# Layer 2 in two passes over halves of DFF, its first product by Strassen's scheme

## The chip, the cores and the metric

The kernel runs on one core of one Trainium2 chip. The metric is the device time of one execution in microseconds. One execution was also taken with the hardware profiler; all rows of the trace are from that one. Its engines are called PE (TensorE), DVE (VectorE), ACT (ScalarE), POOL (GpSimd) and SP (SyncE, which here only issues DMAs).

## The reference, cut to what matters

Attention over 4 x 576 tokens with a memory term gives 2304 tokens of 512. Two layers follow, each a product with a 512 x 2048 matrix, a function of each element, and a product with a 2048 x 512 matrix. The change touches the second of them.

```python
def _moe_ref(x, w_in, w_out, s, b):          # layer 1
    r = np.maximum(x @ w_in, 0.0)
    return (s * (r * r) + b) @ w_out

def _moe2_ref(x, w_in, w_out):               # layer 2
    h = x @ w_in
    g = np.where(h >= 1.0, h, np.where(h <= -1.0, 0.0, (h + 1.0) ** 2 / 4.0))
    return g @ w_out
```

The weights come as 64-bit floats and are converted on the chip.

## The kernel before, in words

**Arithmetic.** Matrix operands are split into a high and a low part of the type float32r (`rnd` rounds, `sub` subtracts the high part), and each product is made of three matmuls: high x high, high x low, low x high. So a product of one 128 x 128 weight tile with a stretch of tokens is three matmuls, each with its own weight load.

**Stages.** Attention and layer 1 are interleaved (`ORDER`, line 44): layer 1 takes blocks of 256 tokens, its last, block 7, has 512. Its output goes to DRAM (`x2d`) and comes back for layer 2. In layer 1 all of layer 1's weights lie in SBUF, in 32 tiles of 512 KB (`wi0` to `wi15`, `wo0` to `wo15`). During block 7 each of them is replaced, as soon as its last reader is done, by the converted and split tile of layer 2 (`fetch_w`, `split_w`). A conversion is one scaling, one step on the low words and two bitwise steps on VectorE (lines 603 to 614).

**Layer 2** (`layer2`, line 953) takes six blocks of 384 tokens (`T2`). For each of 16 tiles of 128 of DFF: the first product in 4 x 3 matmuls of 384 columns into a PSUM bank (`h_mms`, lines 851 to 853), then the bend on two engines (clip on VectorE, L1000; square on ScalarE, L507; maximum on VectorE, L1002; rounding, L522; subtraction, L514), then 3 x 3 matmuls of 512 columns into three banks that collect the output (L1008, L1009, L1012). After the 16th tile these banks go through SBUF to `out`. x for the next block is loaded and split meanwhile into the other half of `xh` and `xl` (`jx`).

**What sets the order.** The program is a list of operations with what they read and write. `Plan` (line 108) places them one by one on the engines' queues by its own table of costs and hand-over times, so that each engine has a fixed order; an operation may be offered to two or three engines (`rnd`: ScalarE, VectorE, GpSimd; `sub`: VectorE, GpSimd). Operations of VectorE on SBUF and those of GpSimd are not planned at the same time; operations that read PSUM are marked `alone` and are free of that rule. Buffers come from a `Pool`; most pools hand out their units in the order of the program. PSUM has 8 banks: four serve the first product in layer 2 and four the output (`hand_over`, line 945). Where the plan has a gap on PE it puts matmuls on zeros (L1035).

```python
953  def layer2(bi):
956      jx = bi % 2
989      for fi in range(NF):
991          h_mms(fi, hs, n, lambda kt: xh2(kt), lambda kt: xl2(kt), ...)
1000         dve(c_dve(n), alone(... tensor_scalar(a_(), hv(), -1.0, 1.0, ALU.max, ALU.min)), [hs], [r], FFN, [r])
```

## Time and profile before

| | us |
|---|---|
| median of 3 runs (lowest, highest) | 1027.61 (1026.58, 1027.63) |
| the profiled execution, its whole time | 1032.56 |
| its span, first to last instruction | 1030.4 |
| PE busy in the span | 1016.9 |
| DVE busy | 578.3 |
| ACT busy | 535.1 |
| POOL busy | 149.9 |

Busy time is the sum of the times at which an engine had an instruction in work. Matmuls overlap in the array, so a PE that is always busy may still be slower than it could be; how fast it goes is read from the distance between the starts of two matmuls. PEld is the weight load that goes with each matmul. A row's "idle before" is the time that the engine stood still ahead of such instructions, with what ended it.

### The profile page before, as it was taken

What the parts mean: (1) busy time and instruction counts of PE and PEld (TensorE: products, weight loads), DVE (VectorE), ACT (ScalarE), POOL (GpSimd) and SP (SyncE); (2) the same over time, 40 slices, a digit from 0 to 9 for tenths busy, and PEclk for the clock granted to TensorE, in tenths of its full rate; (3) what the DMA queues carried; (4) which work ended last, traced back from release to release, by engine and by line L of the source; (5) the groups of instructions that cost most, each with busy time, mean ns of one, the idle gap of its engine ahead of it and who ended that gap; (6) DMA issues with size and microseconds to landing.
All of it is one profiled execution on the core that took longest, in us unless ns stands there. A gap on an engine that the chain in (4) does not pass through costs nothing.

```text
span 1030.4 us, 18179 instructions
## 1 busy us (share of the span) xinstructions
PE 1016.9 (99%) x7100; PEld 901.2 (87%) x7100; DVE 578.3 (56%) x1425; ACT 535.1 (52%) x1246; POOL 149.9 (15%) x249
## 2 busy tenths in 40 slices
PE   7999999999999999999999999999999999999997
PEld 6799998898898898898997889999999999999996
DVE  5899865625645635634888885343343443534433
...
PEclk8999999999999999999999999999999999999999
...
GB/s 310 185 411 31 20 96 147 62 35 80 65 53 76 46 75 62 60 65 22 93 164 152 193 106 133 1 62 1 1 62 1 1 31 1 31 1 1 31 1 31
DMA packets 32630, 77.20 MB, mean 75 GB/s; under 512 B 3232, under 2 KB 12448, under 8 KB 32544
## 3 DMA queue, kind: packets, MB, share of 16 engines
...
## 4 chain that ended last, share of the span: by engine, by line
PE 91%; ACT 4%; DVE 2%; DMA 2%; issue 0%; POOL 0%; SPq 0%; ACTq 0%; POOLq 0%; DVEq 0%
PE hb L851 9%; PE hb L852 9%; PE hb L853 9%; PE ab L726 6%; PE yb L914 5%; PE yb L919 5%; PE yb L915 5%; PE ab L805 4%; PE ab L781 4%; PE ab L1009 4%; PE ab L1008 4%; PE ab L1012 3%; PE ab L852 3%; PE ab L851 3%; PE ab L853 3%; PE yb L1008 3%
## 5 line engine op out<-in xcount | busy, mean ns | idle before, releaser
L851 PE MATMUL hb<-xh,wi 128*128 128x256 f32 (+2 forms) x704 | 217.7, 309 | 0.1
L852 PE MATMUL hb<-xl,wi 128*128 128x256 f32 (+2 forms) x704 | 214.6, 305 | 0.0
L853 PE MATMUL hb<-xh,wi 128*128 128x256 f32 (+2 forms) x704 | 214.4, 305 | 0.0
L507 ACT ACTIVATE r<-r,con 128x384 f32<-128x384 f32 x96 | 59.2, 617 | 201.2 <-DVE r L1000 201.1
L851 PEld LDWEIGHTS hb<-xh,wi 128*128 128x128 f32 x704 | 132.5, 188 | 8.2 <-issue 3.5
L852 PEld LDWEIGHTS hb<-xl,wi 128*128 128x128 f32 x704 | 132.3, 188 | 3.8
L853 PEld LDWEIGHTS hb<-xh,wi 128*128 128x128 f32 x704 | 132.2, 188 | 2.9
L914 PE MATMUL yb<-gg,wo 128*128 128x256 f32 (+1 forms) x396 | 103.0, 292 | 0.6 <-ACT gg L522 0.6
L915 PE MATMUL yb<-gg,wo 128*128 128x256 f32 (+1 forms) x396 | 98.8, 282 | 0.0
L507 ACT ACTIVATE aa<-aa,sm 128x384 f32<-128x384 f32 (+4 forms) x112 | 69.8, 624 | 47.9 <-DVE sm L737 47.6
L522 ACT ACTIVATE g<-r 128x384 fp32r<-128x384 f32 x96 | 50.5, 526 | 67.3 <-DVE r L1002 67.3
L514 DVE TENSOR_TENSOR gg<-rr,gg 128x256 fp32r<-128x256 f32 x100 | 43.9, 440 | 72.9 <-ACT gg L522 55.2
L914 PEld LDWEIGHTS yb<-gg,wo 128*128 128x128 f32 x396 | 74.5, 188 | 8.0 <-issue 3.6
L737 DVE CUSTOM_DVE_ANT_0 aa<-ab,mask 128x512 f32<-128x512 f32 (+3 forms) x112 | 59.1, 554 | 32.8 <-PE ab L726 32.5
L915 PEld LDWEIGHTS yb<-gg,wo 128*128 128x128 f32 x396 | 74.6, 188 | 0.6
L1000 DVE TENSOR_SCALAR r<-hb 128x384 f32<-128x384 f32 x48 | 26.7, 557 | 79.6 <-PE hb L853 79.5
L919 PE MATMUL yb<-gg,wo 128*128 128x256 f32 (+1 forms) x396 | 69.8, 289 | 0.0
L514 DVE TENSOR_TENSOR g<-r,g 128x384 fp32r<-128x384 f32 x92 | 51.0, 554 | 29.6 <-ACT g L522 29.4
L896 ACT ACTIVATE rr<-hb 128x256 f32<-128x256 f32 x97 | 38.7, 399 | 51.7 <-PE hb L853 50.7
L851 PE MATMUL ab<-xh,wi 128*128 128x384 f32 x192 | 64.9, 338 | 0.0
L852 PE MATMUL ab<-xl,wi 128*128 128x384 f32 x192 | 64.9, 338 | 0.0
L853 PE MATMUL ab<-xh,wi 128*128 128x384 f32 x192 | 64.8, 338 | 0.0
...
## 6 DMA issues: line engine op xcount, KB each, us to landing
...
wir<-in_moe_w_in_dram SPq DMA_DIRECT2D x16, 512.0 KB, 10.3
wor<-in_moe_w_out_dram SPq DMA_DIRECT2D x16, 512.0 KB, 10.2
raw<-in_moe_w_in_dram SPq DMA_DIRECT2D x16, 512.0 KB, 4.0
raw<-in_moe_w_out_dram SPq DMA_DIRECT2D x16, 512.0 KB, 3.7
...
```

The lines of the kernel that those rows point to most:

```text
L507: nc.scalar.activation(o(), i(), func, **{a: b() if callable(b) else b for a, b in kw.items()})
L514: ways = [("DVE", c_dve(n), lambda: nc.vector.tensor_tensor(o(), a(), f(hi()), ALU.subtract))]
L522: ways = [("ACT", c_act(n, 0, psum), lambda: nc.scalar.activation(o(), a(), AF.Copy)), ("DVE", c_dve(n, "tt" if psum else "cp"), lambda: n ...
L726: nc.tensor.matmul(zs[x].t[own if t == 4 else slice(0, n), at:at + c1 - c0], qk.t[own, q0:q0 + n], qk.t[own, k0 + c0:k0 + c1], start=True, ...
L737: dve(c_dve(c1 - c0) + 0.02, alone(lambda a=a, s=s, z=zs[x], c0=c0, c1=c1, m0=m0, pi=pi, j=j, at=at, ao=ao: nc.vector.tensor_tensor_reduce ...
L851: nc.tensor.matmul(o, w_in_part(fi, 0)[:, kt, :], x_h(kt), start=kt == 0, stop=False)
L852: nc.tensor.matmul(o, w_in_part(fi, 0)[:, kt, :], x_l(kt), start=False, stop=False)
L853: nc.tensor.matmul(o, w_in_part(fi, 1)[:, kt, :], x_h(kt), start=False, stop=kt == NK - 1)
L914: nc.tensor.matmul(yv(c), w_out_part(fi, 0)[:, cs], gg.t[0], start=fi == 0 and c % k == 0, stop=False)
L915: nc.tensor.matmul(yv(c), w_out_part(fi, 1)[:, cs], gg.t[0], start=False, stop=False)
L919: pe(c_mm(n), lambda c=c, cs=cs, gg=gg, fi=fi: nc.tensor.matmul(yv(c), w_out_part(fi, 0)[:, cs], gg.t[1], start=False, stop=fi == NF - 1 a ...
L1008: nc.tensor.matmul(ys[c].t, gg.t[0][:, cs], w_out_part(fi, 0), start=fi == 0, stop=False)
```

## The change

Layer 2 makes two passes over all tokens, each with one half of DFF. The first pass leaves its sums in DRAM (`yd`), the second adds its own to them and writes `out`. Blocks have 512 tokens, but for one of 256. For a block of 512, two tiles of DFF (256) and the 512 of x are taken as 2 x 2 matrices of half size, and the first product is made by Strassen's scheme in Winograd's form: seven products with sums of quarters of the weights (`prepare` makes them once) and of x (`x2_sums` makes them for every block and pass), and seven additions on VectorE (`plus`). A group is two such pairs, side by side in one PSUM bank. The block of 256 is done as before, with 256 columns (`plain`). The sums of the weights for the second pass are made during the first and put down in DRAM (`w2d`); `bring` loads them over those of the first pass. The passes go through the blocks as 0 1 2 3 4 and 4 1 2 3 0, so that block 4 keeps its x.

```diff
-T2 = 384
+
+HALF = NF // 4
...
-BLOCKS2 = [(i * T2, (i + 1) * T2) for i in range(NTOK // T2)]
+FIRST, SECOND = (0, 1, 2, 3, 4), (4, 1, 2, 3, 0)
+BLOCKS2 = [(0, T)] + [(T + 2 * T * i, T + 2 * T * (i + 1)) for i in range(4)]
...
+    def prepare(p):
+
+        q, later = p % HALF, p >= HALF
+        plan.phase = 1
+
+        def put(k, make):
+
+            nm, i, j = home(q, k)
+            if not later:
+                make(lambda: part(nm, i, j), home_key(q, k), [])
+                return
+            sg = R_STG2.take()
+            make(lambda: sg.t.bitcast(F32R), sg, [sg])
+            dma(lambda: w2d[p, k // 2][:, 512 * j:512 * j + 512], lambda: sg.t, P * 2048, [sg], [f"w2d{p}_{k // 2}"], W2)
+
+        def split(k, a, r):
+            def make(o, key, acq):
+                rnd(lambda: o()[:, 0:256], a, 256, r, [key], W2, acq=acq)
+                sub(lambda: o()[:, 256:512], a, lambda: o()[:, 0:256], 256, r, [key], W2)
+            put(k, make)
+
+        c1, c2 = fetch_2("wi", 2 * p), fetch_2("wi", 2 * p + 1)
+        ta, tb = R_STG2.take(), R_STG2.take()
+
+        def v(x, j):
+            return lambda: x.t[:, 256 * j:256 * j + 256]
+
+        def tt(o, a, b, op, r, w, acq):
+            add([("DVE", c_dve(256), lambda: nc.vector.tensor_tensor(o(), a(), b(), op)),
+                 ("POOL", c_pool(256, "tt"), lambda: nc.gpsimd.tensor_tensor(o(), a(), b(), op))], r, w, W2, acq)
+        tt(v(ta, 0), v(c2, 0), v(c2, 1), ALU.add, [c2], [(ta, 0)], [ta])
+        tt(v(ta, 1), v(ta, 0), v(c1, 0), ALU.subtract, [(ta, 0), c1], [(ta, 1)], [])
+        tt(v(tb, 0), v(c1, 0), v(c2, 0), ALU.subtract, [c1, c2], [(tb, 0)], [tb])
+        tt(v(tb, 1), v(c1, 1), v(ta, 1), ALU.subtract, [c1, (ta, 1)], [(tb, 1)], [])
+        for k, a, r in ((0, v(c1, 0), c1), (4, v(ta, 0), (ta, 0)), (5, v(ta, 1), (ta, 1)), (3, v(c2, 1), c2), (6, v(tb, 0), (tb, 0)),
+                        (1, v(c1, 1), c1), (2, v(tb, 1), (tb, 1)), (7, v(c2, 0), c2)):
+            split(k, a, [r])
+        for i in range(2):
+            st = fetch_2("wo", 2 * p + i)
+            if not later:
+                o, l = (lambda i=i: wo2(q, i, 0)), (lambda i=i: wo2(q, i, 1))
+                rnd(o, lambda st=st: st.t, 512, [st], [home_key(q, 8 + 2 * i)], W2)
+                sub(l, lambda st=st: st.t, o, 512, [st, home_key(q, 8 + 2 * i)], [home_key(q, 9 + 2 * i)], W2)
+                continue
+            for k in (8 + 2 * i, 9 + 2 * i):
+                sg = R_STG2.take()
+                if k % 2 == 0:
+                    hi = sg
+                    rnd(lambda sg=sg: sg.t.bitcast(F32R), lambda st=st: st.t, 512, [st], [sg], W2, acq=[sg])
+                else:
+                    add([("DVE", c_dve(512), lambda sg=sg, st=st, hi=hi: nc.vector.tensor_tensor(sg.t.bitcast(F32R), st.t, hi.t, ALU.subtract)),
+                         ("POOL", c_pool(512, "tt"), lambda sg=sg, st=st, hi=hi: nc.gpsimd.tensor_tensor(sg.t.bitcast(F32R), st.t, hi.t, ALU.subtract))],
+                        [st, hi], [sg], W2, [sg])
+                dma(lambda k=k: w2d[p, k // 2][:, 512 * (k % 2):512 * (k % 2) + 512], lambda sg=sg: sg.t, P * 2048, [sg], [f"w2d{p}_{k // 2}"], W2)
+        plan.phase = None
...
+    def bring(p):
+
+        for k in range(0, 12, 2):
+            nm, i, _ = home(p % HALF, k)
+            dma(lambda nm=nm, i=i: f(parts_t[nm, i]), lambda k=k: w2d[p, k // 2], P * 4096, [f"w2d{p}_{k // 2}"],
+                [f"{nm}h{i}", f"{nm}l{i}"], W2)
...
+            if len(BLOCKS) - 1 in blocks and fi % 3 == 2 and fi < 3 * HALF:
+                prepare(fi // 3)
...
+    def x2_sums(bi):
+
+        def xr():
+            return made["xr"].rearrange("p (c n) -> p c n", c=NK)
+        load_x2(bi, xr)
+        for kt in range(NK):
+            def xv(kt=kt):
+                return xr()[:, kt]
+            add([("ACT", c_act(512, 1), lambda kt=kt, xv=xv: nc.scalar.activation(xv(), xv(), AF.Identity, bias=col(kt))),
+                 ("DVE", c_dve(512, "cp"), lambda kt=kt, xv=xv: nc.vector.tensor_scalar(xv(), xv(), col(kt), None, ALU.add)),
+                 ("POOL", c_pool(512), lambda kt=kt, xv=xv: nc.gpsimd.tensor_scalar(xv(), xv(), col(kt), 1.0, ALU.add, ALU.mult))],
+                ["xr", "cs"], [f"xr{kt // 2}{j}" for j in range(2)], FFN)
+
+        def b(i, j):
+            return lambda: xr()[:, 2 * i:2 * i + 2, T * j:T * j + T]
+
+        def tt(i, j, a, c):
+            o = b(i, j)
+            add([("DVE", c_dve(512), lambda: nc.vector.tensor_tensor(o(), b(*a)(), b(*c)(), ALU.subtract)),
+                 ("POOL", c_pool(512, "tt"), lambda: nc.gpsimd.tensor_tensor(o(), b(*a)(), b(*c)(), ALU.subtract))],
+                ["xr"] + [f"xr{i}{j}" for i, j in (a, c)], [f"xr{i}{j}"], FFN)
+
+        def halves(k, i, j):
+            a, r = b(i, j), ["xr", f"xr{i}{j}"]
+
+            def hi():
+                return xo_all(k, 0).rearrange("p (c n) -> p c n", c=2)
+
+            def lo():
+                return xo_all(k, 1).rearrange("p (c n) -> p c n", c=2)
+            rnd(hi, a, 512, r + [free_of(k)], [f"xo{k}"], FFN)
+            sub(lo, a, hi, 512, r, [f"xo{k}"], FFN)
+        halves(0, 0, 0)
+        tt(0, 0, (0, 1), (0, 0))
+        halves(4, 0, 0)
+        tt(0, 0, (1, 1), (0, 0))
+        halves(5, 0, 0)
+        tt(0, 1, (1, 1), (0, 1))
+        halves(6, 0, 1)
+        halves(1, 1, 0)
+        tt(1, 0, (1, 0), (0, 0))
+        halves(3, 1, 0)
+        halves(2, 1, 1)
...
+    def bend(c, h):
+
+        gh, gl, x = R_G.take(), R_G.take(), R_C.take()
+
+        def tmp():
+            return x.t
+
+        def cv():
+            return c.t
+        src = c if h is None else h
+        clip = lambda: nc.vector.tensor_scalar(tmp(), src.t, -1.0, 1.0, ALU.max, ALU.min)
+        dve(c_dve(512, "cp" if h is None else "tt"), clip if h is None else alone(clip), [src, "wide"], [x], FFN, [x])
+        act(tmp, tmp, AF.Square, 512, ["sb"], [x], FFN, ap=1, scale=0.5, bias=con[:, 4:5])
+        if h is None:
+            dve(c_dve(512), lambda: nc.vector.tensor_tensor(cv(), cv(), tmp(), ALU.max), [x], [c], FFN)
+        else:
+            dve(c_dve(512), alone(lambda: nc.vector.tensor_tensor(cv(), h.t, tmp(), ALU.max)), [h, x], [c], FFN, [c])
+        rnd(lambda: gh.t, cv, 512, [c, "wide"], [gh], FFN, acq=[gh, gl])
+        sub(lambda: gl.t, cv, lambda: gh.t, 512, [gh, c], [gl], FFN)
+        return gh, gl
+
+    def product(group, name):
+
+        k, z = S_OF[name], R_HB.take()
+        for j, q in enumerate(group):
+            def go(q=q, j=j):
+                o = z.t[:, T * j:T * j + T]
+                for kt in range(2):
+                    nc.tensor.matmul(o, sw(q, k, 0, kt), xo(k, 0, kt), start=j == 0 and kt == 0, stop=False)
+                    nc.tensor.matmul(o, sw(q, k, 0, kt), xo(k, 1, kt), start=False, stop=False)
+                    nc.tensor.matmul(o, sw(q, k, 1, kt), xo(k, 0, kt), start=False, stop=kt == 1 and j == 1)
+            pe(6 * c_mm(T), go, [home_key(q, k), f"xo{k}"], [z], FFN, [z] if j == 0 else [])
+        return z
+
+    def strassen(group):
+
+        p1, u2, u3, c22 = (R_C.take() for _ in range(4))
+
+        def plus(o, x, z):
+            dve(c_dve(512), alone(lambda: nc.vector.tensor_tensor(o.t, z.t, x.t, ALU.add)), [z, x], [o], FFN, [o] * (o is not x))
+        z = product(group, "P1")
+        rnd(lambda z=z: p1.t, lambda z=z: z.t, 512, [z, "wide"], [p1], FFN, True, [p1])
+        plus(u2, p1, product(group, "P6"))
+        plus(u3, u2, product(group, "P7"))
+        z = product(group, "P5")
+        plus(c22, u3, z)
+        plus(u2, u2, z)
+        plus(u3, u3, product(group, "P4"))
+        plus(p1, p1, product(group, "P2"))
+        plus(u2, u2, product(group, "P3"))
+        return [(1, 1, c22), (1, 0, u3), (0, 0, p1), (0, 1, u2)]
...
+    def second(group, i, j, gh, gl, ys, first, last):
+
+        for jj, q in enumerate(group):
+            for t in range(2):
+                y = ys[2 * j + t]
+                cs = slice(T * jj + P * t, T * jj + P * t + P)
+
+                def hi(q=q, y=y, cs=cs, jj=jj):
+                    nc.tensor.matmul(y.t, gh.t[:, cs], wo2(q, i, 0), start=first and jj == 0, stop=False)
+                    nc.tensor.matmul(y.t, gh.t[:, cs], wo2(q, i, 1), start=False, stop=False)
+                pe(2 * c_mm(512), hi, [home_key(q, 8 + 2 * i), home_key(q, 9 + 2 * i), gh], [y], FFN, [y] if first and jj == 0 else [])
+        for jj, q in enumerate(group):
+            for t in range(2):
+                y = ys[2 * j + t]
+                cs = slice(T * jj + P * t, T * jj + P * t + P)
+                pe(c_mm(512), lambda q=q, y=y, cs=cs, jj=jj: nc.tensor.matmul(
+                    y.t, gl.t[:, cs], wo2(q, i, 0), start=False, stop=last and jj == 1), [home_key(q, 8 + 2 * i), gl], [y], FFN)
...
+    def layer2(half, bi, same):
+        p0, p1 = BLOCKS2[bi]
+        ny = (p1 - p0) // P
+        if half:
+            parts = [R_STG2.take() for _ in range(ny)]
+            for c in range(ny):
+                dma(lambda c=c: parts[c].t, lambda c=c: yd[bi][c], P * DM * 4, [f"yd{bi}_{c}"], [parts[c]], W2, [parts[c]])
+        if not same:
+            if bi:
+                x2_sums(bi)
+            else:
+                x2_plain()
+        ys = [R_Y.take() for _ in range(ny)]
+        for g in range(2):
+            group = (2 * g, 2 * g + 1)
+            if bi:
+                for x, (i, j, c) in enumerate(strassen(group)):
+                    gh, gl = bend(c, None)
+                    second(group, i, j, gh, gl, ys, g == 0 and x < 2, g == 1 and x > 1)
+            else:
+                plain(group, g, ys)
+        for c in range(ny):
+            if not half:
+                st = R_STG.take()
+                rnd(lambda st=st: st.t, lambda c=c: ys[c].t, DM, [ys[c]], [st], FFN, True, [st])
+                dma(lambda c=c: yd[bi][c], lambda st=st: st.t, P * DM * 4, [st], [f"yd{bi}_{c}"], FFN)
+                continue
+            st = parts[c]
+            dve(c_dve(DM), alone(lambda c=c, st=st: nc.vector.tensor_tensor(st.t, ys[c].t, st.t, ALU.add)), [ys[c]], [st], FFN)
...
+    for x, bi in enumerate(FIRST):
+        layer2(0, bi, False)
+        if x < HALF:
+            prepare(HALF + x)
+            plan.phase = 1
+    for p in range(HALF, 2 * HALF):
+        bring(p)
+    for x, bi in enumerate(SECOND):
+        layer2(1, bi, x == 0)
```

Left out are the new plumbing of buffers (the unused weight tiles 12 to 15 of layer 1 become temporaries of layer 2), the split of `fetch_w` into `convert` and two callers, and the deleted body of `layer2`.

## Rows read from the trace of the kernel before

**Rows 1.** The page's parts 1 and 2: busy us by engine; 40 slices of the span.

```profile
PE 1016.9 (99%) x7100; PEld 901.2 (87%) x7100; DVE 578.3 (56%) x1425; ACT 535.1 (52%) x1246; POOL 149.9 (15%) x249
...
PEclk8999999999999999999999999999999999999999
...
GB/s 310 185 411 31 20 96 147 62 35 80 65 53 76 46 75 62 60 65 22 93 164 152 193 106 133 1 62 1 1 62 1 1 31 1 31 1 1 31 1 31
```

**Rows 2.** PE's own waits: us in total, times, longest us.

```profile
PE ab L726 <- DMA wir<-in_qk_dram: 4.2, 1, 4.2
...
PE hb L1035 <- DVE zr L547: 1.1, 1, 1.1
```

**Rows 3.** Busy us (xcount): window, length, PE, PEld, DVE, ACT, POOL; clock, DMA share, GB/s.

```profile
545.00:605.00 60.00, 60.00 (x258) 48.21 (x257) 50.61 (x74) 39.43 (x68) 21.53 (x26) 1.00 0.54 173
...
660.00:1000.00 340.00, 340.00 (x1706) 309.13 (x1705) 143.59 (x260) 99.73 (x176) 12.32 (x16) 1.00 0.05 17
```

**Rows 4.** Groups of matmuls by line and shape: busy us, mean ns | idle before.

```profile
L851 PE MATMUL ab<-xh,wi 128*128 128x384 f32 x192 | 64.9, 338 | 0.0
...
L851 PE MATMUL hb<-xh,wi 128*128 128x384 f32 x192 | 64.9, 338 | 0.0
...
L1008 PE MATMUL ab<-wo,g 128*128 128x512 f32 x160 | 62.8, 393 | 0.0
...
L1008 PE MATMUL yb<-wo,g 128*128 128x512 f32 x128 | 50.3, 393 | 0.1
```

**Rows 5.** Timeline of PE in layer 2, 640 to 646 us: start us, us.

```profile
639.81 0.34 PE L851 MATMUL ab<-xh,wi 128*128 128x384 f32 x1
...
642.99 0.34 PE L851 MATMUL hb<-xh,wi 128*128 128x384 f32 x1
...
643.52 0.39 PE L1008 MATMUL ab<-wo,g 128*128 128x512 f32 x1
...
645.82 0.39 PE L1009 MATMUL ab<-wo,g 128*128 128x512 f32 x1
```

**Rows 6.** Busy time in three stretches of layer 1 with 256-column matmuls alone.

```profile
57.00:117.00 60.00, 59.46 (x500) 58.29 (x499) 56.28 (x110) 59.73 (x144) 11.20 (x16) 1.00 0.38 152
...
220.30:229.60 9.30, 9.30 (x84) 9.30 (x83) 1.49 (x4) 4.48 (x12) 0.41 (x1) 1.00 0.01 2
...
504.00:527.50 23.50, 23.12 (x203) 22.93 (x203) 22.00 (x37) 14.13 (x34) 6.17 (x6) 1.00 0.54 181
```

**Rows 7.** Timeline of DVE and POOL in block 7; between the last two, three operations.

```profile
606.21 0.66 POOL L605 TENSOR_SCALAR st<-raw 128x512 f32<-128x512 f32 x1 [0.54 <-DMA raw<-in_moe_w_in_dram]
...
606.25 1.15 DVE L514 TENSOR_TENSOR g<-xr,g 128x512 fp32r<-128x512 f32 x1
...
607.33 0.68 DVE L614 SCALAR_TENSOR_TENSOR st<-raw,st 128x512 uint32<-128x512 uint32 x1
...
609.74 0.68 DVE L612 SCALAR_TENSOR_TENSOR st<-st,raw 128x512 uint32<-128x512 uint32 x1
```

**Rows 8.** Groups of elementwise work of 512 columns on DVE and ACT.

```profile
L523 DVE COPY st<-yb 128x512 f32<-128x512 f32 x3 | 2.1, 692 | 5.7 <-PE yb L1012 5.7
...
L604 DVE TENSOR_SCALAR st<-raw 128x512 f32<-128x512 f32 x3 | 1.3, 427 | 0.1
...
L507 ACT ACTIVATE aa<-aa,sm 128x512 f32<-128x512 f32 x32 | 23.0, 721 | 6.4 <-DVE sm L737 6.4
...
L522 ACT ACTIVATE wo<-st 128x512 fp32r<-128x512 f32 x13 | 8.2, 634 | 13.4 <-PE ab L919 13.4
```

**Rows 9.** Timeline of PE and DVE at the end: the last tile of DFF.

```profile
1019.41 0.55 DVE L1000 TENSOR_SCALAR r<-hb 128x384 f32<-128x384 f32 x1
...
1021.14 0.61 PE L1035 MATMUL ab<-zr 128*128 128x128 f32 x4
...
1021.88 0.50 PE L1008 MATMUL yb<-wo,g 128*128 128x512 f32 x1
```

**Rows 10.** DMA issues: KB each, median us to landing.

```profile
xr<-x2d SPq DMA_DIRECT2D x5, 512.0 KB, 4.0
```

239 lines of the change are left out of this document (131 added, 108 removed).

## The prediction

> **What bounds the kernel now.** I began with the page's totals and slices: TensorE is busy 1016.9 of 1030.4 us, at the full granted clock in every slice but the first, and after the opening DMA moves far less than the 411 GB/s that its best slice shows [rows 1]. Next the waits of TensorE alone: what the trace can name is 4.2 us for the first load and 1.1 us at the start; nothing else reaches 1 us [rows 2]. So one engine sets the time, and only its work or new gaps in it can move the end. A busy TensorE may still be slow, since matmuls overlap, so I read its rate as the distance from one matmul's start to the next. Two windows give the climate: block 7 of layer 1 (512 tokens, with layer 2's weights converted beside it) has VectorE busy 50.6 of 60 us and ScalarE 39.4, and TensorE does not pause; in layer 2 VectorE is busy 143.6 of 340 us, 42%, and DMA is nearly idle [rows 3]. Layer 2 therefore has spare VectorE time to pay with. That is the coin that this change spends.
>
> **Matmuls removed and added.** Before, layer 2's first product is 6 blocks x 16 tiles of DFF x 12 matmuls of 384 columns = 1152 (three source lines, each 192 + 192), and the second 6 x 16 x 9 = 864 of 512 columns (three lines, each 160 + 128) [rows 4]. Starts of 384-column matmuls lie 18 steps in 642.99 - 639.81 = 3.18 us, 176.7 ns; of 512, ten steps in 2.30 us, 230 ns [rows 5]. The two products are then 1152 x 0.1767 = 203.6 us and 864 x 0.230 = 198.7 us; nothing else of size stands on TensorE there.
>
> After: a group is two pairs of DFF tiles. For a 512-token block each of seven products takes 12 matmuls of 256 columns, 84 a group; 4 blocks x 4 groups give 1344. The 256-token block is done plainly: 8 pairs x 24 = 192. Together 1536 of 256 columns, 393,216 columns for 442,368: one eighth less on eight ninths of the tokens. The second product keeps its 864 matmuls of 512.
>
> What does a 256-column matmul take? Layer 1 shows it, in stretches with no other matmuls, two or three of each count having begun before the window: 9.3 us / 81 = 114.8 ns where VectorE is nearly idle; 23.5 / 200 = 117.5 ns where it is busy 22.0 of 23.5 us; 60 / 497 = 120.7 ns where ScalarE never rests either [rows 6]. These include small waits for operands. Per column 256 is thus no worse than 384 (0.449 to 0.472 against 0.460 ns), although twice as many weight loads stand per column as at 512. I take 118 for pass 1, whose VectorE load I find below to be near that of the second row, and 116 for pass 2: 768 x 0.118 + 768 x 0.116 = 179.7 us. Gain 203.6 - 179.7 = **23.9 us**; ends 1536 x 0.1148 = 176.3 (gain 27.3) and 1536 x 0.1207 = 185.4 (gain 18.2).
>
> [...]
>
> The 512-column matmuls took 230 ns in the quiet layer 2 and 60 / 256 = 234.4 ns in block 7 beside weight traffic [rows 3, 5]. Pass 1 gets such traffic, pass 2 little: 432 x 0.0044 = **1.9 us lost**; ends 0 and 3.8. Block 7 of layer 1 loses half of its conversions (16 weight tiles, not 32): at best 384 x 0.0044 = 1.7 us gained; I take 0.5.
>
> **Elementwise work added.** Per group VectorE gets 7 additions that read PSUM, and 4 bends (clip, ScalarE square, maximum, rounding on ScalarE, subtraction) of 512. A 512 operation on PSUM lasts 692 ns, a clip of an SBUF source about as long as 427 [rows 8]; queued back to back, 512-column operations start 2.41 us / 4 = 0.60 us apart [rows 7]. Per 512-token block and pass: 14 additions x 0.60 = 8.4, 8 bends x (0.43 + 0.60 + 0.60) = 13.0, the seven operands of x with 7 subtractions and 4 differences x 0.60 = 6.6: 28.0 us. In pass 1 each block also carries one pair's weights for pass 2 (`prepare`): 8 weight steps, 2 subtractions of 512 and 12 of 256, 10 x 0.60 + 12 x 0.34 (an estimate, half of 0.60 and a little) = 10.1. So 38.1 us of VectorE against TensorE's 2 x (84 x 0.118 + 48 x 0.234) = 42.3 us: 90% if GpSimd takes nothing, though it is offered the SBUF subtractions. Over the whole pass it is less, since four pairs are spread over five blocks: 4 x 38.1 + 9 for block 0, 161 of 192 us, 84%. In pass 2 the partial result is added on VectorE, 4 x 0.60: 30.4 of 42, 73%. ScalarE needs, at 0.63 to 0.72 each [rows 8], about 16 for bends, 13 for x and evictions, 8 for weights: under 40 of 42 even by busy time, which overlaps. Block 7 shows such a load beside a TensorE that does not pause [rows 3], so I cost this work at nothing; its cover is the 42 us of matmuls, and without that it costs its excess, which is the first rival.
>
> **The new orders and waits.** (1) x's operands have one buffer. The next block's operand k can be written only when this block's product P_k has read it in its second group, and the differences are made in place, so the chain runs through all seven: 7 x (0.63 + 0.69) + 4 x 0.69 = 12.0 us, some 15 with hand-overs. It can run from P5's end, the fourth product; before the next block's last product TensorE still has 3 products (4.2 us), the group's second products (11.2) and 6 products (8.5), 24 us in all. Hidden, at six hand-overs. (2) At layer 1's end the bends wait for block 7's last matmul, since their buffers are its weights, and VectorE's later operations queue behind the first clip. Block 0's four first products (96 x 0.1175 = 11.3 us) are free of that wait and cover the first bend, 0.69 + 0.72 + 0.69 + 0.63 = 2.7 us and hand-overs. Block 1's x is also loaded only then (4.0 us to land for 512 KB [rows 10]) and its 15 us chain ends some 19 us after layer 1; block 0 has 11.3 + 48 x 0.234 = 22.5 us, a few of which may be spent early, and the last operand is wanted 8.5 us after the first. (3) Between the passes 24 weight tiles of 512 KB come back over those just used, each load on SP's queue waiting for its tile's last reader; the loads of x and of partial sums queue behind it. The first group's 8 first-product tiles have one group's first product and two groups' second ones, about 9.9 + 2 x 11.2 = 32 us; 4.2 MB need 10 us at 411 GB/s and 24 us at block 7's 173 [rows 1, 3]. Hidden. (4) Partial sums go out and back, 18 x 256 KB each way, in slack. (5) The end: the last bend of 512 takes longer than the old one of 384 (clip start to the next matmul 1019.41 to 1021.88 = 2.47 us, filled by the previous tile's matmuls up to 1021.14; 0.74 us were lost [rows 9]), but 12 instead of 9 matmuls of the previous pair fill it, 2.76 us. No change.
>
> No row shows (1) to (3) at work, so I bound their sum by 0 and by 8 us, about one unhidden landing (4 us) at each of the two changes of stage; a gain is excluded, as TensorE has no named wait there to win back. I take **4 us**, the middle: block 7 ran a like load without a pause, but with some points less on VectorE than 90%.
>
> **Sum**, against the profiled execution of 1032.56 us (span 1030.4 and 2.2 around it): -23.9 + 1.9 - 0.5 + 4 = -18.5, so 1014.1. That execution lies 4.95 us above the median of 1027.61; on the median's scale 1009.1, say **1009**. With all ends: -29.0 gives 998.6, -18.2 + 3.8 + 8 = -6.4 gives 1021.
>
> **Rivals.** *VectorE becomes the bound of pass 1, and the kernel is slower.* Beside a GpSimd operation a VectorE operation of SBUF takes 1.15 us and not 0.68, and the next starts 1.08 later and not 0.60 [rows 7]: 0.48 lost. From 38.1 us, nine such a block bring VectorE to TensorE's 42.3; with 19 it is 47.2 and the whole gain is lost; with 25, 50.1, 8 us over in 4 blocks, 32 us: time **1041**. For: block 7 had 26 GpSimd operations in 60 us [rows 3], 18 in 42, and there VectorE had less to do. Against: a subtraction that GpSimd takes spares VectorE 0.60 for the 0.48 that it may cost; and block 7's 84% hold the stretched ones already.
> *The chain of x is not hidden.* If the bends' VectorE work of a group (4 x 1.81 = 7.2 us) goes ahead of it and its steps run at 1.15, it is 7 x 1.78 + 4 x 1.15 + 3 + 7.2 = 27.3 us against 24: 3.3 us at six places, 20 us, and nothing is left: **1027**. It decides from 24 us on. Against: bends are spread over the group.
> *The exchange of weights is not hidden.* If writes and other loads leave 100 GB/s, the first 4.2 MB need 42 us for 32, and the second group's the same: 10 to 14 us lost, **1018 to 1022**. Against: DMA stands at a share of 0.05 in layer 2 [rows 3].
> *The columns do not fall as the source says*: hardly possible, the matmuls are written out one by one; 1%.
>
> **How the numbers follow.** Forecast 69%; exchange 9%, still faster; chain of x 7%, of which 5 within and 2 faster; VectorE 14%, slower; the columns 1%, within. About 0.2% (2 us) is what a measurement of this kernel can tell from no change. Faster 0.80, same 0.06, slower 0.14. The range 999 to 1023 takes the forecast's ends and the exchange.
>
> **What would show it.** After: 1536 matmuls of 256 in layer 2 at 115 to 119 ns a step; VectorE at 8 to 9 tenths in pass 1 and 6 to 7 in pass 2; no named TensorE wait over 2 us there; one DMA burst between the passes, ended before its tiles are read. Wrong if TensorE waits in a row for VectorE in pass 1 (first rival), for x's operands at block changes (second), for weights at mid-layer (third), or if the steps at 256 are nearer to 121.

## The result, and the profile after

The changed kernel takes 1016.63 us (median of 4 executions, 1014.98 to 1018.43) where the kernel before takes 1027.62 beside it: a ratio of 0.9887 with a 95% interval of 0.9858 to 0.9917, so 11 us or 1.1% faster. The forecast was 1009, with a range of 999 to 1023. The direction and the range held; the gain is 11 us and not 18.5.

The profiled execution took 1018.43 us, 14.1 less than that of before; the one of before lies 4.95 us above its median, this one only 1.80, which is why 14.1 stands beside 11. The first lines of its page (busy us by engine; 40 slices of the span), against [rows 1]:

```profile
span 1016.6 us, 19496 instructions
...
PE 998.8 (98%) x7484; PEld 882.8 (87%) x7484; DVE 679.8 (67%) x1597; ACT 571.0 (56%) x1301; POOL 192.3 (19%) x298
...
PE   8999999999999999999999999999999999989997
...
DVE  5999855625744635644878967988797458666753
...
PEclk8999999999999999999999999999999999998999
```

TensorE is still the engine that sets the end, and VectorE got 101 us more to do. New is a dip near the end of the line of TensorE, and one in the line of the granted clock. TensorE's own waits say where (us in total, times, longest), against [rows 2]:

```profile
PE yb L1202 <- ACT wo L536: 5.2, 2, 3.6
PE ab L1171 <- POOL xx L532: 2.4, 1, 2.4
PE ab L825 <- DMA wir<-in_qk_dram: 2.0, 2, 1.2
PE hb L1298 <- DVE zr L561: 1.1, 1, 1.1
```

Before, nothing but the first load and the start was named. Now layer 2 has three waits: two of the second product (L1202) for a bend's rounded result, one of the first product (L1171) for an operand of x. The windows (length, PE, PEld, DVE, ACT, POOL busy with xcount; clock, DMA share, GB/s) are pass 1, the exchange of the weights, the rest of pass 2, and two stretches at a wait; [rows 3] is the level of before:

```profile
620.00:784.00 164.00, 161.65 (x1044) 147.32 (x1043) 138.00 (x228) 88.08 (x153) 45.60 (x48) 0.99 0.48 163
784.00:826.00 42.00, 42.00 (x263) 37.88 (x262) 23.37 (x41) 14.27 (x24) 2.02 (x2) 1.00 0.84 304
826.00:1000.00 174.00, 168.81 (x1028) 151.12 (x1027) 113.95 (x186) 55.16 (x90) 20.07 (x20) 0.98 0.19 58
...
719.20:722.60 3.40, 3.40 (x10) 2.62 (x10) 3.40 (x7) 1.24 (x2) 0.00 (x0) 0.50 0.00 0
913.70:920.50 6.80, 6.09 (x14) 4.80 (x15) 6.77 (x11) 3.71 (x6) 1.06 (x1) 0.50 0.00 1
```

The last two rows are stretches at a granted clock of 0.50, called the half clock below: 3.4 us after the wait at 715, 6.8 us at the one at 910, of which the first 0.7 are still wait (6.09 of 6.80 busy). A 512-column step takes 427 ns in them and 227 elsewhere; summed over their steps this cost 4.6 us. The steps at a granted clock of 1.00, TensorE's timeline (start us, us), once for the first product and once for the second:

```profile
905.82 0.28 PE L1171 MATMUL ab<-xx,wi 128*128 128x256 f32 x1
...
910.06 0.28 PE L1171 MATMUL ab<-xx,wi 128*128 128x256 f32 x1
```

```profile
699.66 0.39 PE L1203 MATMUL ab<-wo,wo 128*128 128x512 f32 x1
...
701.47 0.39 PE L1203 MATMUL yb<-wo,wo 128*128 128x512 f32 x1
```

Between the first two are 36 steps: 4.24 us / 36 = 117.8 ns, and 118 is also the median of all 256-column steps of layer 2, in both passes. Between the second two are 8 steps: 1.81 / 8 = 226 ns, median 227, where [rows 5] gave 230. The means, without the long steps, are 228.3 after and 229.7 before.

Where the 14.1 us went, by TensorE's timeline:

| | before | after | difference |
|---|---|---|---|
| layer 2's first matmul starts at | 621.35 | 618.84 | -2.5 |
| first product, steps of layer 2 | 1152 x 0.1767 = 203.6 | 1536 x 0.118 = 181.2 | -22.4 |
| second product, steps of layer 2 | 864 x 0.2297 = 198.5 | 864 x 0.2283 = 197.3 | -1.2 |
| steps over 25 ns longer than their median, the excess summed | 0.6 | 13.8 | +13.2 |
| from the last matmul to the end of the execution | 8.7 | 7.7 | -1.1 |

The sum is -14.0 for -14.1 measured. Steps run from the start of one matmul to the start of the next; matmuls on zeros that fill a gap are taken off. The -2.5 is mostly the wait for the first load, 4.2 before and 2.0 here; between 1.5 and 2.9 in the runs below, it belongs to no part of the change. The 13.8 is three long gaps with 8.1 (2.6, 1.7 and 3.8), 4.6 at the half clock, and small ones. Below, a gap is given as the whole distance between the two starts around it: 2.7, 1.9 and 3.9. So the matmuls gave what they should, and the new orders took a good half of it back.

What stood ahead of each gap? ScalarE (ACT), VectorE and TensorE around 866 and 911 us, timeline with the idle time before an instruction and its releaser; these are the changes from block 1 to 2 and 2 to 3 in pass 2:

```profile
861.67 0.72 ACT L521 ACTIVATE wif<-wif,con 128x512 f32<-128x512 f32 x1 [10.11 <-DVE wif L1152]
865.59 0.72 ACT L1106 ACTIVATE xr<-xr,cs 128x512 f32<-128x512 f32 x1 [3.19 <-DMA xr<-x2d]
866.22 0.71 ACT L521 ACTIVATE wof<-wof,con 128x512 f32<-128x512 f32 x1
866.83 0.71 ACT L1106 ACTIVATE xr<-xr,cs 128x512 f32<-128x512 f32 x1
867.44 0.61 ACT L536 ACTIVATE wo<-wof 128x512 fp32r<-128x512 f32 x1
...
868.63 0.50 PE L1202 MATMUL yb<-wo,wo 128*128 128x512 f32 x1 [1.59 <-ACT wo L536]
```

```profile
910.96 1.33 ACT L1106 ACTIVATE xr<-xr,cs 128x512 f32<-128x512 f32 x2 [4.80 <-DMA st<-yd]
912.20 0.70 ACT L521 ACTIVATE wof<-wof,con 128x512 f32<-128x512 f32 x1
912.81 0.61 ACT L536 ACTIVATE wo<-wif 128x512 fp32r<-128x512 f32 x1
...
912.94 0.69 DVE L1156 TENSOR_TENSOR wof<-wof 128x512 f32<-128x512 f32 x1 [5.04 <-ACT wof L521]
```

L1106 is the bias step on the next block's x; L521 and L536 are the square and the rounding of the bends that the second product needs now. ScalarE stands for 3.19 and 4.80 us at a bias step whose x has not landed, with the square of a bend queued behind it. (The second row names a load of partial sums as what ended the wait. The step reads only x and the column sums; the second half of x was issued at 905.60 and took 5.3 us to land, to 910.89, 0.07 us before the step.) Nobody needs that x so soon: the next block's first product starts at 879.7 and 928.3 us. The bend is needed at once. SP's queue shows when x was asked for (issues of DMAs; last, in a view of its own, KB and us to landing of the one issued at 905.60):

```profile
852.79 0.37 SPq L510 DMA_DIRECT2D xr<-x2d  x1
853.51 2.68 SPq L510 DMA_DIRECT2D out_dram<-st  x4
858.96 0.92 SPq L510 DMA_DIRECT2D st<-yd  x2
859.97 0.38 SPq L510 DMA_DIRECT2D out_dram<-st  x1
860.41 0.43 SPq L510 DMA_DIRECT2D xr<-x2d  x1
...
905.60 0.42 SPq L510 DMA_DIRECT2D xr<-x2d  x1
```

```profile
xr<-x2d SPq DMA_DIRECT2D x1, 512.0 KB, 5.3
```

x comes in two halves. The second is issued 7.6 us after the first, since loads of partial sums (`st<-yd`), the last two of the block before, stand between them and wait for their buffers to go out. That an earlier issue would have brought x in time is not shown: no run below got it in earlier. The gap at 715 has the same shape on another engine: GpSimd (POOL) stands at a step on weights for pass 2 until their DMA lands, and behind it is x's low half, for which TensorE waits:

```profile
715.20 0.85 POOL L598 TENSOR_SCALAR raw<-raw 128x512 int32<-128x512 uint32 x1 [2.00 <-DMA raw<-in_moe_w_out_dram]
716.13 3.02 POOL L532 TENSOR_TENSOR xx<-xr,xx 128x512 fp32r<-128x512 f32 x2
...
717.76 0.39 PE L1171 MATMUL ab<-xx,wi 128*128 128x256 f32 x1 [2.35 <-POOL xx L532]
```

### The profile page after: what moved, and what is told of

Read it like the earlier page. It is cut to its first block, busy times and chain, and to the rows that moved or that the text cites. A ratio compares the mean times of both kernels' runs of the same rounds, so it can differ in the third digit from the quotient of the medians.

```text
span 1016.6 us, 19496 instructions
## 1 busy us (share of the span) xinstructions
PE 998.8 (98%) x7484; PEld 882.8 (87%) x7484; DVE 679.8 (67%) x1597; ACT 571.0 (56%) x1301; POOL 192.3 (19%) x298
## 4 chain that ended last, share of the span: by engine, by line
PE 86%; ACT 8%; DMA 3%; DVE 1%; issue 1%; SPq 0%; POOL 0%; DVEq 0%; ACTq 0%; POOLq 0%
PE hb L950 6%; PE hb L952 6%; PE hb L951 6%; PE ab L825 6%; PE yb L1013 5%; PE yb L1018 5%; PE yb L1014 5%; PE ab L904 4%; PE ab L880 4%; PE ab L1202 3%; PE yb L1202 3%; PE ab L1203 3%; PE yb L1203 3%; PE yb L1209 3%; PE ab L1209 3%; PE hb L1170 2%
## 5 line engine op out<-in xcount | busy, mean ns | idle before, releaser
L950 PE MATMUL hb<-xx,wi 128*128 128x256 f32 (+1 forms) x512 | 152.7, 298 | 0.1
L951 PE MATMUL hb<-xx,wi 128*128 128x256 f32 (+1 forms) x512 | 149.6, 292 | 0.0
L952 PE MATMUL hb<-xx,wi 128*128 128x256 f32 (+1 forms) x512 | 149.6, 292 | 0.0
L950 PEld LDWEIGHTS hb<-xx,wi 128*128 128x128 f32 x512 | 96.3, 188 | 7.1 <-issue 3.5
L951 PEld LDWEIGHTS hb<-xx,wi 128*128 128x128 f32 x512 | 96.4, 188 | 2.8
L952 PEld LDWEIGHTS hb<-xx,wi 128*128 128x128 f32 x512 | 96.2, 188 | 2.9
L528 DVE TENSOR_TENSOR gg<-rr,gg 128x256 fp32r<-128x256 f32 (+1 forms) x105 | 46.2, 442 | 76.0 <-ACT gg L536 56.4
L521 ACT ACTIVATE aa<-aa,sm 128x384 f32<-128x384 f32 (+4 forms) x112 | 69.4, 621 | 48.6 <-DVE sm L836 48.4
L521 ACT ACTIVATE wif<-wif,con 128x512 f32<-128x512 f32 x46 | 33.1, 721 | 87.4 <-DVE wif L1152 87.3
L1013 PEld LDWEIGHTS yb<-gg,wo 128*128 128x128 f32 x394 | 74.1, 188 | 7.4 <-issue 3.6
L1014 PEld LDWEIGHTS yb<-gg,wo 128*128 128x128 f32 x394 | 74.2, 188 | 0.4
L994 ACT ACTIVATE rr<-hb 128x256 f32<-128x256 f32 (+1 forms) x102 | 40.9, 401 | 56.7 <-PE hb L952 55.5
L825 PE MATMUL ab<-qk 64*64 64x512 f32 (+5 forms) x320 | 58.3, 471 | 0.0
L1018 PEld LDWEIGHTS yb<-gg,wo 128*128 128x128 f32 x394 | 54.5, 188 | 2.2 <-issue 1.8
L1171 PE MATMUL ab<-xx,wi 128*128 128x256 f32 x192 | 54.1, 282 | 2.4 <-POOL xx L532 2.4
L1170 PE MATMUL ab<-xx,wi 128*128 128x256 f32 x192 | 54.0, 281 | 0.0
L1170 PE MATMUL hb<-xx,wi 128*128 128x256 f32 x192 | 54.0, 281 | 0.0
L1171 PE MATMUL hb<-xx,wi 128*128 128x256 f32 x192 | 54.0, 281 | 0.0
## 6 DMA issues: line engine op xcount, KB each, us to landing
wir<-in_moe_w_in_dram SPq DMA_DIRECT2D x16, 512.0 KB, 10.2
```

The source lines that it names most:

```text
L521: nc.scalar.activation(o(), i(), func, **{a: b() if callable(b) else b for a, b in kw.items()})
L825: nc.tensor.matmul(zs[x].t[own if t == 4 else slice(0, n), at:at + c1 - c0], qk.t[own, q0:q0 + n], qk.t[own, k0 + c0:k0 + c1], start=True, ...
L950: nc.tensor.matmul(o, w_in_part(fi, 0)[:, kt, :], x_h(kt), start=kt == 0, stop=False)
L951: nc.tensor.matmul(o, w_in_part(fi, 0)[:, kt, :], x_l(kt), start=False, stop=False)
L952: nc.tensor.matmul(o, w_in_part(fi, 1)[:, kt, :], x_h(kt), start=False, stop=kt == NK - 1)
L1013: nc.tensor.matmul(yv(c), w_out_part(fi, 0)[:, cs], gg.t[0], start=fi == 0 and c % k == 0, stop=False)
```

## The experiments

Theory H (head of a queue): the lost time is a step that waits for a DMA at the head of an engine's in-order queue, with urgent steps behind it. Rival C: the chain that makes x's operands in their single buffer is too long in itself. Rival V: VectorE has too much to do, and the gaps are where that shows. All edits start from the changed kernel; the diffs are cut to what matters. The kernel's planner makes every engine's order anew after each edit, so the trace has to show where a step went. Ratios are to the kernel before, run beside each.

| run | us | ratio, 95% |
|---|---|---|
| the changed kernel | 1016.63 | 0.9887 [0.9858, 0.9917] |
| e1: bias on x on GpSimd alone | 1006.98 | 0.9796 [0.9778, 0.9813] |
| e1 again | 1007.02 | 0.9791 [0.9770, 0.9812] |
| e6: bias on ScalarE alone | 1016.76 | 0.9876 [0.9849, 0.9903] |
| e11: bias on VectorE alone | 1016.68 | 0.9909 [0.9893, 0.9926] |
| e2: landings planned 3 us later | 1009.81 | 0.9822 [0.9807, 0.9837] |
| e5: e1 and e2 | 1010.71 | 0.9822 [0.9793, 0.9851] |
| e7: more buffers for partial sums | 1013.78 | 0.9854 [0.9818, 0.9891] |
| e8: e7 and e1 | 1007.54 | 0.9788 [0.9762, 0.9814] |
| e9: x's loads first on SP | 1010.32 | 0.9818 [0.9794, 0.9841] |
| e10: e9 and e1 | 1006.95 | 0.9784 [0.9759, 0.9810] |
| e3: no second half of the weights | 1014.34 | 0.9869 [0.9846, 0.9892] |
| e4: two passes, no Strassen | 1037.02 | 1.0087 [1.0068, 1.0106] |

**The bias step on one engine: e1, e6, e11.** Each keeps one of the three engines that the planner may choose from in `x2_sums`; e1's edit, with ACT's or DVE's line in place of POOL's for the others:

```diff
-            add([("ACT", c_act(512, 1), lambda kt=kt, xv=xv: nc.scalar.activation(xv(), xv(), AF.Identity, bias=col(kt))),
-                 ("DVE", c_dve(512, "cp"), lambda kt=kt, xv=xv: nc.vector.tensor_scalar(xv(), xv(), col(kt), None, ALU.add)),
-                 ("POOL", c_pool(512), lambda kt=kt, xv=xv: nc.gpsimd.tensor_scalar(xv(), xv(), col(kt), 1.0, ALU.add, ALU.mult))],
+            add([("POOL", c_pool(512), lambda kt=kt, xv=xv: nc.gpsimd.tensor_scalar(xv(), xv(), col(kt), 1.0, ALU.add, ALU.mult))],
```

> The first step of x's sums (adding the column sums to the freshly loaded x) is offered to GpSimd alone; ScalarE and VectorE no longer take it. Theory H (head of a queue): TensorE's waits at the two block changes of the second pass come from ScalarE, where this step waits for x's DMA ahead of a bend's square. Then both gaps (1.9 and 3.9 us) and the 6.8 us at half clock behind the second go, about 1.8 + 3.8 + 3.4 = 9 us: 1007 to 1010 us; the 2.7 us gap of the first pass stays. Theory C (the chain of x's sums is too long): TensorE waits at the same places for x's operands instead, same size or larger: 1016 to 1022 us. Theory V (VectorE is the bound): within 1 us of 1016.6.

> The opposite of the first experiment: the first step of x's sums on ScalarE alone, so all four steps of a block that wait for x's DMA stand in the queue of the bends' squares. Theory H: the gaps at block changes stay or grow, as ScalarE is held until x has landed at every one: 1017 to 1026 us. Theory C (length of the chain): four steps of 0.71 us one after the other instead of two beside two on GpSimd make the chain 1.4 us longer, no more than 1.4 us a gap: 1016 to 1021 us, with TensorE's waits on x's operands, not on the bends. If ScalarE's queue does not matter: 1014 to 1018 us.

> The bias step on x on VectorE alone, which carries each bend's clip, maximum and subtraction. Head of an in-order queue that also holds the bends: x's late landing now stops VectorE, and the second products wait for VectorE or for what follows it, 2 us or more at changes of block of pass 2, half clock after some of them: 1012 to 1020 us. If GpSimd helps only because ScalarE had too much to do, VectorE (about 63 to 79 per cent busy in layer 2) takes the steps as well as GpSimd: 1005 to 1009, no TensorE wait over 1.5 us in layer 2. If VectorE's free time is what is short (32 more steps of about 0.43 us), many waits under 1 us in pass 1 and no large ones.

e1 gives 1006.98, at the lower end of what H expected, and 1007.02 when run again. One part of the expectation failed: the gap at 715, which was to stay, is gone. TensorE's waits in e1, where layer 2 holds only the second line (1.2 us in two):

```profile
PE ab L825 <- DMA wir<-in_qk_dram: 2.1, 2, 1.1
PE ab L1207 <- DVE wo L528: 1.2, 2, 0.8
PE hb L1296 <- DVE zr L561: 1.1, 1, 1.1
```

No half clock is left in layer 2, and the excess over the steps falls from 13.8 to 3.9 us: 9.9, beside 9.7 us between the medians. Not all of it is due to the bias step. The two gaps of pass 2 and their half clock were worth 8.5, which the edit aimed at; the gap at 715 and its half clock another 4.2, which went since the new order of GpSimd's queue has no late weight there; and new small gaps cost some 3. The bias step itself became slower. Its row in e1, and below it that in e6 (ns min/median/max, first and last start):

```profile
L1106 POOL TENSOR_SCALAR xr<-xr,cs x24: 690/908/1738, 654.1 to 911.4; 128x512 f32<-128x512 f32 x24
```

```profile
L1106 ACT ACTIVATE xr<-xr,cs x24: 706/708/727, 657.3 to 915.4; 128x512 f32<-128x512 f32 x24
```

The rows hold the 24 steps from 640 us on. In e1 their median is 908 ns in place of 708; of all 28, 15 take 690 to 707 and 13 take 852 to 1738, and each of the slow ones has VectorE at work on SBUF beside it. So the chain of x's operands got longer, and the kernel is faster. That speaks against C: a longer chain should have cost. With all of them on ScalarE (e6) the gaps of pass 2 are there, ScalarE's timeline and TensorE's wait:

```profile
912.43 0.72 ACT L1106 ACTIVATE xr<-xr,cs 128x512 f32<-128x512 f32 x1 [6.75 <-DMA st<-yd]
913.06 0.70 ACT L521 ACTIVATE wif<-wif,con 128x512 f32<-128x512 f32 x1
```

```profile
PE yb L1200 <- ACT wo L536: 6.8, 2, 5.2
```

x's second half landed at 912.07, so here too it is x that the step waited for, though the row names another load. The changed kernel has 13 of the 24 on ScalarE, two of four at each of these changes of block. The gap at 715 is gone in e6 though nothing aimed at it: the planner put GpSimd's steps elsewhere. A new wait of 1.4 us ends at 677, some 5 us after ScalarE had stood 2.77 us at a step on weights that waited for their load, with the squares of two bends behind it. So the time, 1016.76, does not judge here: it lies just under H's 1017 and within the other cases. TensorE's wait does, which is for a bend and not for x.

e11 settles whether ScalarE is special. VectorE takes the step in 476 ns, the fastest of the three. Its timeline at 902 to 909 us, and TensorE's waits:

```profile
902.39 0.68 DVE L1179 TENSOR_TENSOR wof<-hb,wof 128x512 f32<-128x512 f32 x1
908.61 0.49 DVE L1106 TENSOR_SCALAR xr<-xr,cs 128x512 f32<-128x512 f32 x1 [5.54 <-issue]
909.01 0.42 DVE L1150 TENSOR_SCALAR wif<-wof 128x512 f32<-128x512 f32 x1
```

```profile
PE yb L1200 <- ACT wo L536: 5.1, 1, 5.1
PE ab L825 <- DMA wir<-in_qk_dram: 2.3, 2, 1.5
PE hb L1169 <- POOL xx L532: 1.7, 1, 1.7
```

VectorE stands 5.54 us at the bias step, with the clip of a bend (L1150) behind it. The row names no releaser; x's second half landed at 908.53, 0.08 us before the step. TensorE then waits 5.1, by its row for ScalarE, whose square of that bend stood idle for 6.24 us until the clip at 909.01 was done. The half clock follows (6.8 us). Where the step shares a queue with the bends, a late x stops the bends. On GpSimd in e1 x lands at 863.26 and 907.11, within half a microsecond of where it landed before against TensorE's own progress, but at the changes of block of pass 2 that queue holds only x's own steps:

```profile
863.45 4.34 POOL L1106 TENSOR_SCALAR xr<-xr,cs 128x512 f32<-128x512 f32 x4 [21.05 <-DMA xr<-x2d]
867.77 0.61 POOL L541 TENSOR_SCALAR xx<-xr 128x512 fp32r<-128x512 f32 x1
```

It waits as the others do, and stops nobody. H stands for pass 2: with the bias off the bends' queues (e1, e1 again, e8, e10) the kernel takes 1007.0 to 1007.5, with it in them (e6, e11, the changed kernel) 1016.6 to 1016.8. What the gaps of pass 2 are worth by themselves is read better from e9 below, where they go and the gap at 715 stays: 6 to 7 us. That it is ScalarE's load that GpSimd relieves falls, since VectorE, faster at the step, doesn't relieve it as well.

**Landings planned later: e2 and e5.** The planner reckons a DMA as landed 1.3 us after its transfer. e2 makes that 4.3 for layer 2's loads, so that what needs them is queued later; e5 is that with e1's edit.

```diff
-                o.ends = ("SP", dma + self.DMA_END)
+                o.ends = ("SP", dma + self.DMA_END + self.LATE * (o.pr == 4))
```

with LATE = 3.0.

> The planner believes that every transfer of layer 2 lands 3 us later than it believed before; nothing else is changed, so work that needs a transfer is queued later and ahead of it stands other work. Theory H: all three gaps of TensorE in layer 2 (2.7, 1.9, 3.9 us) go, with both stretches at half clock (3.4 and 6.8 us), some 13 us: 1002 to 1007 us. Theory C: the chain still has its length, the gaps stay: 1014 to 1020 us. Theory V: 1014 to 1018 us.

> Both edits together: the first step of x's sums on GpSimd alone, and the planner's belief in 3 us later landings. Theory H (head of a queue): the former leaves gaps of 1.2 and 0.8 us in the first pass, behind work that waits for weight loads; the latter should take these too: 1004 to 1007 us. If instead the later belief only moves work to worse places, 1008 to 1011 us, as with it alone.

e2 gives 1009.81: nearly 7 us of the 9.6, no half clock in layer 2, but four gaps of 0.4 to 1.7 us, an excess of 5.9. A later place in the queue thus helps without any change of engine, as H says, but less than expected: at the change at 909 ScalarE again stood 5.17 us at a bias step, ahead of a bend's rounding. e5, 1010.71, misses what H expected, lies in the other case, and is worse than e1: the later plan made a gap of 2.9 us at 915 with 3.4 us of half clock. ScalarE's timeline there:

```profile
916.30 0.63 ACT L536 ACTIVATE xx<-xr 128x512 fp32r<-128x512 f32 x1 [7.29 <-POOL xr L1106]
916.84 0.61 ACT L536 ACTIVATE g<-wof 128x512 fp32r<-128x512 f32 x1
```

This is the head of a queue once more, one step further on: ScalarE stands at the rounding of x's first operand until GpSimd has done the bias, and behind it is the rounding of a bend, for which TensorE waits 2.5 us. Taking the bias out of the bends' queues is enough only where the next step on x stands late enough in them.

**Buffers for partial sums: e7 and e8.** In pass 2 SP's queue stood at `st<-yd` loads, 24.7 us in 12 waits for an output's landing. e7 gives blocks 1 and 3 other buffers, in the weights' staging that is idle by then; e8 is e7 with e1's edit.

```diff
+    R_PART = Pool([lambda j=j, h=h: f(made[f"raw1{j}"])[:, h * DM:(h + 1) * DM] for j in range(3) for h in range(2)])
...
-            parts = [R_STG2.take() for _ in range(ny)]
+            parts = [(R_PART if bi % 2 else R_STG2).take() for _ in range(ny)]
...
-                dma(lambda c=c: parts[c].t, lambda c=c: yd[bi][c], P * DM * 4, [f"yd{bi}_{c}"], [parts[c]], W2, [parts[c]])
+                dma(lambda c=c: parts[c].t, lambda c=c: yd[bi][c], P * DM * 4, [f"yd{bi}_{c}"] + [f"w2d{p}_{k}" for p, k in w2d] * (bi % 2), [parts[c]], W2, [parts[c]])
```

The last line makes these loads wait until the weights staged there have gone out.

> ScalarE keeps its steps of x's sums; instead the buffers for the partial sums of the second pass are doubled (every other block loads them into the idle weight-load buffers), so that on SP's queue their loads no longer wait for the stores of the block before, ahead of the second half of x's load. If SP's order makes x late: x is issued some microseconds earlier, the gaps of 1.9 and 3.9 us in the second pass and the 6.8 us at half clock go: 1006 to 1010 us. If x is late only because its transfer takes longer than planned: the gaps stay within 1 us of their size: 1014 to 1018 us.

> The doubled buffers together with the first step of x's sums on GpSimd alone. Theory H: the second pass has nothing left to lose, so it adds little to the first experiment: 1005 to 1008 us. More than 2 us below that experiment would say that late transfers also cost elsewhere.

e7, 1013.78, lies between its two expectations and is inconclusive: SP's queue still stood behind outputs, x's second half was still issued 7.6 and 9.2 us after the first (850.87 to 858.51, 894.70 to 903.88), and the three gaps stayed at 2.7, 2.0 and 2.9 us. It did not take away what it aimed at. e8 equals e1.

**x's loads ahead on SP: e9, e10, and e1 again.** `x2_sums` is called before the loads of the same block's partial sums, and these name x's buffer among what they follow, so that both halves of x are issued ahead of them. e10 adds e1's edit.

```diff
-        if half:
-            parts = [R_STG2.take() for _ in range(ny)]
-            for c in range(ny):
-                dma(lambda c=c: parts[c].t, lambda c=c: yd[bi][c], P * DM * 4, [f"yd{bi}_{c}"], [parts[c]], W2, [parts[c]])
         if not same:
             if bi:
                 x2_sums(bi)
             else:
                 x2_plain()
+        if half:
+            parts = [R_STG2.take() for _ in range(ny)]
+            for c in range(ny):
+                dma(lambda c=c: parts[c].t, lambda c=c: yd[bi][c], P * DM * 4, [f"yd{bi}_{c}", "xr"], [parts[c]], W2, [parts[c]])
```

> At a change of block of pass 2 the loads of the next x are issued ahead of the loads of the stored partial sums, so that x's second half no longer stands on SP's queue behind a partial sum that waits for an output's landing. ScalarE keeps the bias steps. If that order of SP's queue makes x late for the bias step at the head of ScalarE's queue: TensorE's two waits of 2 to 4 us at the changes of block of pass 2 go, the half clock after them too, the gap at 715 us stays: 1006 to 1010 us. If x's transfer itself, begun only when the single buffer is free, is what is too late: x's second half is issued right behind the first, and yet the bias step still holds back the bends, gaps over 1.5 us stay there, 1013 to 1018.

> x's loads ahead of the partial sums' and the bias steps on GpSimd alone. Head of a queue: ScalarE no longer waits for x at all, so the order of SP's queue has little left to give: 1005 to 1008, within 2 us of the kernel with the bias on GpSimd alone that runs beside it. If late x also costs by another way than ScalarE's queue, this one is faster than that by 2 us or more.

> The bias on x on GpSimd alone once more, on the same chip as the two kernels with another order of loads: 1006 to 1008 again, no wait of TensorE over 1.5 us in layer 2 and no half clock there. If the first run of it was a lucky one: 1010 or more.

e9 gives 1010.32. SP's queue and ScalarE's at the same change of block as above:

```profile
861.51 1.22 SPq L510 DMA_DIRECT2D xr<-x2d  x2
...
871.39 0.63 ACT L536 ACTIVATE g<-wif 128x512 fp32r<-128x512 f32 x1 [0.80 <-DVE wif L1156]
871.93 1.32 ACT L1106 ACTIVATE xr<-xr,cs 128x512 f32<-128x512 f32 x2
```

Both halves go out together, but at 861.5, a microsecond after the second half went before: two loads of the previous block's partial sums, issued at 858.7 and 860.1, still stood ahead of them. x lands at 869.12, later than the 865.50 of the changed kernel. What changed is the order of the steps that need it: two of the four bias steps are on GpSimd, which has nothing else to do there, and ScalarE's two now stand behind the block's last bends and start without idle time. Both gaps of pass 2 are gone, with the steps on the same two engines; the gap at 714 (3.0 us and 6.8 us of half clock) stays, as expected, and is most of the excess of 7.5. So the expectation's result came true by a way that it did not name: not an earlier x, but a later place of the step that needs it. e10 (1006.95) and e1 beside it (1007.02) agree: with the bias out of the bends' queues, this order of loads gives nothing. What an earlier x would give stays untested, since neither e7 nor e9 made it earlier.

**The weights of pass 2 left out: e3.** Nothing is converted in pass 1 for pass 2, and no weights are exchanged (`prepare` for the second half and `bring` are not called); pass 2 computes with the first half's weights.

> Left out: the making of the second half's weights in the first pass, with its loads and its writes to DRAM, and the exchange between the passes; the second pass computes with the first half's weights. Theory H: the gap of the first pass (2.7 us, behind a GpSimd step that waits for a weight load) and its 3.4 us at half clock go, 4.3 us; the two gaps of the second pass stay: 1011 to 1014 us. Theory V: the first pass has been held up by VectorE all along and gains more than 10 us: under 1006 us. Theory C: the gap in the first pass stays: 1015 to 1018 us.

1014.34, only 2.3 us less, and just above H's 1011 to 1014. The gap at 715 is gone, as its late weight is; those of pass 2 stay, at 2.4 and 5.2 us (1.9 and 3.9 before), and the excess is 10.2 for 13.8. The wait is again that for a bend:

```profile
PE yb L1202 <- ACT wo L536: 7.0, 2, 4.9
```

The first product's step is still 118 ns. V falls, and with it the thought that conversions and exchange are what keeps the kernel from 1009.

**No Strassen: e4.** Layer 2 in two passes over nine plain 256-token blocks, 1728 matmuls of 256 columns for the first product.

```diff
-FIRST, SECOND = (0, 1, 2, 3, 4), (4, 1, 2, 3, 0)
-BLOCKS2 = [(0, T)] + [(T + 2 * T * i, T + 2 * T * (i + 1)) for i in range(4)]
+FIRST, SECOND = tuple(range(9)), (8, 1, 2, 3, 4, 5, 6, 7, 0)
+BLOCKS2 = [(T * i, T * i + T) for i in range(9)]
...
```

Every block then goes through `x2_plain` and `plain`.

> The two passes without Strassen's scheme: nine blocks of 256 tokens, each done plainly, 1728 matmuls of 256 columns in the first product instead of 1536. At 118 ns that is 192 x 0.118 = 22.7 us more on TensorE. Theories H and C: without the in-place sums of x there is slack everywhere, the 13 us of gaps and half clock go: 1016.6 + 22.7 - 13 = 1026 us; with the gaps it would be 1039 us. Theory V: VectorE loses a third of its work and more than the gaps goes: under 1024 us.

1037.02, 9.4 us above the kernel before and near the case "with gaps" of the expectation. Its first product is 1728 x 0.1167 = 201.7 us of steps (the mean; a quarter of them take 113 or 114 ns), little less than the 203.6 before; the excess is 9.3 us, 59 small gaps and none above 1.1. So the two passes by themselves save next to nothing on the matmuls and cost small gaps, and the seven products give 20 us beside the changed kernel, 30 beside e1.

## Why the prediction was right, and where it was not

**The matmuls.** The step of the argument that carries the gain held: 1536 matmuls of 256 columns, predicted at 116 to 118 ns, at 118; -22.4 us for -23.9. The choice of 116 for pass 2, because VectorE has less to do there, was wrong in its reason: pass 2 steps at 118 as pass 1 does. The second product, 512 columns, was to lose 1.9 from more weight traffic and gained 1.2.

**VectorE's load** was foreseen at 84% in pass 1 and 73% in pass 2 (its 30.4 of 42 is 72); the windows show 138.0 of 164 us, 84%, and 114.0 of 174, 65%. It is no bound: the first rival (1041) did not happen, and e3, which takes the work on pass 2's weights away, is only 2.3 us faster.

**The stalls of the new orders are the term that was mis-sized:** 4 us, bounds 0 and 8; measured 13.2, of which e1 wins 9.9 back, most of it but not all by the bias step. Two things are in it. First, step (1) was argued as a chain: how long x's seven operands take, against how long TensorE can go on. That chain is hidden at the changes of block of pass 2; TensorE waited there for bends, not for x. What the step left out is that a chain's first link sits in a queue in which other work must pass: ScalarE stood 3.19, 4.80 and in e6 6.75 us, VectorE in e11 5.54, each with a bend behind. In the traces the bend's step does not go ahead of the bias step: around 911 in the changed kernel the bend's clip, started at 906.04 us, took 0.43, and its square started only at 912.20, behind two bias steps at 910.96; in e6 the clip started at 905.55 and took 0.43, and the square started at 913.06, behind the bias step at 912.43; in e11 the last sum on VectorE started at 902.39 and took 0.68, and the clip started at 909.01, behind the bias step at 908.61. The prediction itself reckoned with such an order for VectorE at layer 1's end, and for SP ("the loads of x and of partial sums queue behind it"), but put a price on neither engine that does the bias nor on SP's loads of partial sums ahead of x; step (4) called those "in slack", and they split x's two halves by 7.6 us, though what that split cost is not shown. Second, the bound of 8 counted landings and not what follows: 4.6 us went at the half clock at the gaps. The kernel before shows this once, which the prediction passed over: around the end of the 4.2 us wait for the first load [rows 2] the granted clock is 0.51, from 11.5 to 18.4 us, and the first slice of PEclk in [rows 1] is an 8 for it.

**How the terms add up.** Of the 7.6 us between forecast and median, 3.1 are the scale: the forecast carried the 4.95 us between profiled execution and median over from before, and here it is 1.80. The other 4.4 are -18.5 forecast for -14.1 measured: 9.2 too little for the stalls and 1.5 too much for the first product, against 3.1 better in the second product and 3.1 in the start and the end, which held 0.5 in the forecast. These last two were luck: no argument foresaw them, and without their 6.2 us the time would have been near 1023, the end of the range.

**The rivals.** The second, the chain of x, is seen once, at 715, with 2.4 us and not six times 3.3; and there too GpSimd's queue stood behind a late weight; with that weight left out (e3) the gap is gone. The third, the exchange of weights, did not happen: from 784 to 826 the DMA is at a share of 0.84 and 304 GB/s, between my 173 and 411, and TensorE is busy for all 42.0 us.

**"What would show it"** gave: steps of 115 to 119 (right), VectorE at 8 to 9 and 6 to 7 tenths (right over each pass, 84% and 65%; single slices run from 7 to 9 and from 4 to 8), one burst of DMA at mid-layer (right), no wait over 2 us (wrong, one of 2.4 and one of 3.6). With that last one made true, by e1, the kernel takes 1007, 2 us under the forecast of 1009. The forecast was that of a kernel with 4 us of stalls, and e1 has 3.9; the changed kernel's orders are not as well placed. The version of e1 (or e10, equal to it) takes 2.0% to 2.2% less than the kernel before.
